# Scores of the first step's last pair of heads: sums over masked keys in place of gathered rows

## The chip, the core and the metric

The kernel runs on one core of a Trainium2 chip. The metric is the device time of one execution in microseconds (us).

The engines are PE (TensorE, matmuls), DVE (VectorE), ACT (ScalarE), POOL (GpSimd) and SP (SyncE, which here only issues DMA transfers). Each works through its own instructions in a fixed order, and waits where a result of another is missing.

## The reference

What is computed is a gated linear attention over 4 batches, 8 heads, 768 positions and 48 channels, followed by a layer of two matrix products:

```
f = 1 / (1 + exp(-f_logit))
for t in range(S):
    state = f[t][:, None] * state + outer(k[t], v[t])      # per batch and head, 48 x 48
    y[t] = q[t] @ state
x = y, all heads side by side                              # 3072 x 384
h = x @ w_in                                               # 384 -> 2048
g = where(h >= 1, h, where(h <= -1, 0, (h + 1) ** 2 / 4))
out = g @ w_out                                            # 2048 -> 384
```

The weights arrive as 64-bit floats, the rest as 32-bit.

## The kernel before, in words

**Steps and pairs.** The 768 positions are cut into 6 steps of C = 128 (`NI`). In each, the heads go by pairs (`NP` = 4): a pair has head 0 in partitions 0 to 47 and head 1 in 64 to 111. The first three pairs have one tile each, `kq[0]` to `kq[2]`, with keys in columns 0 to 511 and queries behind them. Partitions 48 to 63 and 112 to 127 of these tiles are free, and the fourth pair lies there, in thirds of 16 channels. `move` gathers those thirds by six DMA transfers into the tile `kq[3]`, half of them issued by SP and half by ACT.

**Gates.** `gate(m)` prepares one of three tiles per step (`NT` = 3): ACT takes the sigmoid; DVE runs a scan over the gates backwards (the tile `w`, line 471), takes its last column with a lower clamp of 1e-30 (`end`, line 474), its reciprocal (`rec`, 477), runs a scan forwards (478), and multiplies keys (480) and queries (482) by the two scans. The first tile of step 0 goes in two halves. POOL multiplies `end` by the first gate for a test of the range that the kernel makes (`least`, lines 494 and 496).

**Step 0.** It has no state yet, so its outputs are masked scores times values. `scores(n)` (594) makes, for pair n, the products of keys and queries of both heads in two PSUM banks, and two products on DVE with the mask (600) give `am`. `heads(t)` (821) and `thirds(t)` (832) multiply these by the values and gather x tile t in the bank `firsts[t]`: `heads` for the pairs' own heads, `thirds` for the pieces of the fourth pair. `rounded` (673 on ACT, 674 on DVE) writes each x as a sum of two reduced floats. `transpose_tensor` (654, with a copy to `kn` on ACT, 657) and `states` (762) prepare the state for step 1.

**Units.** The layer has 96 units, 16 (`NJ`) per step. `unit_1(k)` makes 128 rows of h for 512 columns by nine matmuls (236; for unit 0 line 863), ACT and DVE form g and split it (`act_1`, `act_2`, `act_3`, `ghi`, `glo`: 239, 242, 247, 250, 253), and `unit_2(k)` adds nine matmuls to the three output banks `po` (260), one unit behind.

**Weights.** `split_piece(k)` loads a piece of the weights into one of three buffers `raw`, and makes of it a high and a low part: ACT 364, DVE 366 (`bits`), ACT 369 (`w_hi`), DVE 370 (`w_lo`). A piece's load waits for line 366 of the piece three before. Units 0 to 3 have pieces of their own.

**What sets the order.** All this is written down as operations with costs and dependencies; `Plan.order` makes a list of it by a simulation with its cost table, and every engine, SP's DMA queue too, gets its instructions in that order. Where the plan leaves PE idle for more than 500 ns, `warm` (314) puts in matmuls of zeros, called fill here. Two tables, `TURNS` and `VISITS`, say beside which units the work of the later steps is put. The first step's work is put in by the lines 944 to 957 and 976 to 983.

## Time and profile before

| | |
|---|---|
| three runs | 484.01, 485.67 and 486.31 us; median 485.67 |
| the profiled execution | 484.96 us |
| its span, first to last instruction | 483.1 us |
| PE busy | 473.1 us (98%) |
| DVE busy | 372.5 us (77%) |
| ACT busy | 263.2 us (54%) |
| POOL busy | 22.1 us (5%) |
| HBM read | 44.63 MB |

All profile rows come from the profiled execution and are counted from the start of its span. Busy times of PE include fill. A timeline row that stands for several instructions gives their number behind the x; where they overlap, the time is that of all together. A matmul of 32-bit floats appears as two records. The middle column of a wait in brackets is the engine's idle time before the instruction, and what ended it.

### The profile page before, as it was taken

The page shows a single profiled execution, that of the slowest core. Times are in us where ns is not written, and L with a number is a line of the kernel's source. Part 1 is how long each engine was busy: PE and PEld are TensorE (multiplying, and loading weights), DVE is VectorE, ACT ScalarE, POOL GpSimd, SP SyncE. Part 2 cuts the span into 40 slices and gives each one's busy share as a digit, 9 for nine tenths or more (in the row PEclk, how much of TensorE's full clock was granted, in tenths as well). Part 3 has the DMA queues.
Part 4 walks back from the last instruction along what each step waited for, and adds up shares of the span by engine and source line. Part 5 has one row for each costly group of instructions (what it writes and reads, how often), then busy time and mean ns, then how long its engine had stood idle before and what let it go on. Part 6 is the DMA issues. An engine that isn't in the chain of part 4 may idle for free.

```text
span 483.1 us, 11267 instructions
## 1 busy us (share of the span) xinstructions
PE 473.1 (98%) x4664; PEld 385.1 (80%) x4664; DVE 372.5 (77%) x737; ACT 263.2 (54%) x483; POOL 22.1 (5%) x54
## 2 busy tenths in 40 slices
PE   8999999999999999999999999999999999999994
PEld 3678888889987887888887878888888888888883
DVE  7999878865899999999999589877667555655532
ACT  2489898754645455455555436464545444544451
POOL 3100001000100010110002000101000000000000
PEclk9999999999999999999999999999999999999998
DMA  8888644206502143013241413233410243422201
GB/s 305 262 305 294 229 136 144 73 3 231 156 2 89 68 117 96 31 36 121 88 127 39 152 45 122 67 109 79 152 45 3 88 114 96 156 86 86 85 0 71
DMA packets 21866, 54.48 MB, mean 113 GB/s; under 512 B 3472, under 2 KB 6672, under 8 KB 21808
## 3 DMA queue, kind: packets, MB, share of 16 engines
q1 hardware_dynamic: 20464, 51.53, 33.0%
q10 hardware_dynamic: 1344, 2.17, 1.9%
q8 instruction: 38, 0.62, 0.5%
q14 instruction: 20, 0.16, 0.1%
HBM read 44.63 MB, written 4.72 MB: 102 GB/s over the span
## 4 chain that ended last, share of the span: by engine, by line
PE 82%; DVE 7%; DMA 6%; ACT 2%; issue 1%; SPq 0%; DVEq 0%; ACTq 0%
PE po L260 38%; PE ph L236 36%; DMA raw<-in_w 5%; DVE kn L668 2%; PE pa L690 2%; PE pa L722 2%; PE ph L635 1%; DMA act<-in_f 1%; DVE act L247 1%; DVE w L471 1%; PE ph L783 1%; DVE glo L253 1%; PE pa L783 1%; ACT bits L364 1%; DVE f L478 1%
## 5 line engine op out<-in xcount | busy, mean ns | idle before, releaser
L236 PE MATMUL ph<-x,w_hi 128*128 128x512 f32 (+1 forms) x606 | 146.4, 377 | 0.0
L239 ACT ACTIVATE act<-ph,half 128x512 f32<-128x512 f32 x96 | 66.0, 687 | 115.8 <-PE ph L236 112.9
L236 PEld LDWEIGHTS ph<-x,w_hi 128*128 128x128 f32 x606 | 109.6, 188 | 21.1
L247 DVE SCALAR_TENSOR_TENSOR act<-ph,act 128x512 f32<-128x512 f32 x96 | 66.0, 687 | 59.9 <-ACT act L242 59.4
L250 ACT CAST ghi<-act 128x512 fp32r<-128x512 f32 x96 | 59.6, 621 | 66.2 <-DVE act L247 64.2
L260 PE MATMUL po<-ghi,w_hi 128*128 128x512 f32 (+1 forms) x306 | 87.0, 389 | 0.9 <-ACT ghi L250 0.8
L260 PE MATMUL po<-glo,w_hi 128*128 128x512 f32 (+1 forms) x306 | 83.5, 378 | 0.1
L260 PE MATMUL po<-ghi,w_lo 128*128 128x512 f32 (+1 forms) x306 | 83.4, 378 | 0.0
L236 PE MATMUL ph<-x,w_lo 128*128 128x512 f32 (+1 forms) x303 | 81.2, 376 | 0.0
L253 DVE TENSOR_TENSOR glo<-act,ghi 128x512 fp32r<-128x512 f32 x96 | 65.9, 686 | 16.0 <-ACT ghi L250 14.6
L668 DVE STREAM_TRANSPOSE kn<-kq 32x128 f32<-32x128 f32 x224 | 67.8, 303 | 3.5
L260 PEld LDWEIGHTS po<-glo,w_hi 128*128 128x128 f32 x306 | 55.3, 188 | 11.6 <-DVE glo L253 0.7
L260 PEld LDWEIGHTS po<-ghi,w_lo 128*128 128x128 f32 x306 | 55.4, 188 | 10.9
L236 PEld LDWEIGHTS ph<-x,w_lo 128*128 128x128 f32 x303 | 55.3, 188 | 10.4
L260 PEld LDWEIGHTS po<-ghi,w_hi 128*128 128x128 f32 x306 | 53.3, 188 | 12.4 <-ACT ghi L250 2.3
L242 ACT ACTIVATE act<-act 128x512 f32<-128x512 f32 x96 | 60.7, 632 | 3.0
L380 DVE TENSOR_REDUCE ok<-raw 128x1 f32<-128x512 f32 x48 | 31.3, 679 | 4.8 <-DMA raw<-in_w 4.8
L364 ACT ACTIVATE bits<-raw,top_of 128x512 uint32<-128x512 fp8e4 (+1 forms) x25 | 18.4, 742 | 9.7 <-DMA raw<-in_w 9.6
L471 DVE TENSOR_TENSOR_SCAN w<-f,ones 128x512 f32<-128x512 f32 (+1 forms) x21 | 21.3, 1016 | 2.4 <-ACT f L469 2.1
L478 DVE TENSOR_TENSOR_SCAN f<-f,rec 128x512 f32<-128x512 f32 (+1 forms) x21 | 21.3, 1020 | 0.5
L569 ACT ACTIVATE sd<-sd,kq 112x48 f32<-112x48 f32 x80 | 19.9, 327 | 0.0
L494 POOL TENSOR_TENSOR kq<-end,f0s 128x4 f32<-128x4 f32 (+1 forms) x21 | 4.9, 233 | 306.8 <-DVE end L474 227.4
(99 smaller groups left out, 377.7 us busy)
## 6 DMA issues: line engine op xcount, KB each, us to landing
raw<-in_w SPq DMA_DIRECT2D x24, 512.0 KB, 3.5
raw<-in_w SPq DMA_DIRECT2D x21, 511.6 KB, 4.4
kq<-in_kq SPq DMA_DIRECT2D x18, 512.0 KB, 4.9
out_y<-raw SPq DMA_DIRECT2D x18, 256.0 KB, 2.2
v<-in_v SPq DMA_DIRECT2D x10, 384.0 KB, 5.5
f<-in_f SPq DMA_DIRECT2D x13, 256.5 KB, 3.2
raw<-in_w SPq DMA_DIRECT2D x4, 382.9 KB, 5.4
kq<-kq SPq DMA_DIRECT2D x15, 64.2 KB, 3.0
```

The lines of the kernel that those rows point to most:

```text
L236: nc.tensor.matmul(ps[:, to], w_in(w_hi if high else w_lo, j, kt), xt[:, kt, t, c], start=(n == 0), stop=(n == 8))
L239: nc.scalar.activation(a, ps, AF.Relu, bias=half, scale=0.5)
L242: nc.scalar.activation(a, a, AF.Square)
L247: nc.vector.scalar_tensor_tensor(out=a, in0=ps, scalar=1.0, in1=a, op0=ALU.max, op1=ALU.min)
L250: nc.scalar.copy(hi, a)
L253: nc.vector.tensor_tensor(out=lo, in0=a, in1=hi.bitcast(F32), op=ALU.subtract)
L260: nc.tensor.matmul(po[e][:, c], w_out(part, j, e), g[:, of], start=(j == 0 and n == 0 and c.start == 0), stop=(j == NJ - 1 and n == 2))
L364: m = sca(COST["act"] * n // W, lambda: nc.scalar.activation(t, top, AF.Abs, bias=top_of, scale=2.0 ** 30), loaded, made[k - 4] if k >= 4 ...
L380: seen.append(vec("dve", lambda z=z, op=op: nc.vector.tensor_reduce(out=ok[:, 1 + NG + z + c:2 + NG + z + c], in_=words_of(raw[2])[1].bitc ...
L471: s1 = vec(1200 // count, lambda bwd=bwd, u0=u0, u1=u1: nc.vector.tensor_tensor_scan(out=wide(w[:, u0:u1]), data0=bwd, data1=wide(ones[:, ...
L478: s2 = vec(1200 // count, lambda fwd=fwd, b0=b0, b1=b1: nc.vector.tensor_tensor_scan(out=fwd, data0=fwd, data1=wide(rec[:, b0:b1]), initia ...
L668: nc.vector.transpose(kn[n % 2][u:u + 32, ::-1, r:r + 32], src[:, :, u:u + 32])
```

## The change

Four things change.

The last pair of step 0 gets its scores in another way. Its keys and queries are no longer gathered first. `scores_of_last(t)` lets ACT copy the keys of tile t with a scale that is 1 in the partitions of the last pair's thirds and 0 elsewhere (an extra column of `f0s`, which the host fills), and multiplies 32 rows of the copy, from partition 32 and from 96, with the queries of the same rows. The masked rows add nothing, and the sums over t = 0, 1, 2 gather in two banks. The copies lie in `kn`, which is free so early. The moves of step 0 take only the keys (512 columns, not 1028) and no longer wait for POOL.

Masks are an operation of their own (`masks`), and two tables, `START` and `AFTER`, set in which order the first step's operations are given to the plan. The transposes of pairs 0 and 1 come behind unit 0, those of pairs 2 and 3 behind unit 2's first layer. Banks and mask tiles are dealt out anew for this: pair 2 uses the second `ph` bank, in which fill was written, so no fill follows its scores until the units run.

The clamp becomes part of the first scan: where it multiplied and added a row of ones and zeros, it multiplies and takes the maximum with a row that holds 1 at a block's start and 1e-30 elsewhere. DVE's line 474 goes; the reciprocal reads `w` itself, and POOL copies the last column to `end`.

`TURNS` and `VISITS` are written out as tables; their numbers are the same.

```diff
+START = (("scores", 0), ("mask", 0), ("last", 0), ("scores", 1), ("mask", 1), ("last", 1), ("scores", 2), ("last", 2), ("mask", 2),
+         ("first", 0), ("first", 1), ("mask", 3), ("second", 3), ("second", 0), ("second", 1), ("second", 2))
+AFTER = {0: (("turn", 0), ("turn", 1)), 1: (("states", 0),), 2: (("turn", 2), ("turn", 3)), 3: (("states", 2),)}
...
-    def start_ones():
-        nc.vector.memset(ones, 0.0)
-        nc.vector.memset(ones[:, :, 0], 1.0)
+    def start_least():
+        nc.vector.memset(least_w, 1e-30)
+        nc.vector.memset(least_w[:, :, 0], 1.0)
...
             s1 = vec(1200 // count, lambda bwd=bwd, u0=u0, u1=u1: nc.vector.tensor_tensor_scan(
-                out=wide(w[:, u0:u1]), data0=bwd, data1=wide(ones[:, u0:u1]), initial=0.0,
-                op0=ALU.mult, op1=ALU.add), sg, None if split_up else c["sg"], set_ones, last)
-            en = vec("small", lambda b0=b0, b1=b1, u0=u0, u1=u1: nc.vector.tensor_scalar(
-                out=et[:, b0:b1], in0=w[:, u1 - 1:(u0 - 1 if u0 else None):-1, C - 1], scalar1=1e-30, scalar2=None, op0=ALU.max),
-                s1, of_half(m - 2, o, "pf"))
-            rc = vec("small", lambda b0=b0, b1=b1: nc.vector.reciprocal(out=rec[:, b0:b1, 0], in_=et[:, b0:b1]), en, last, set_rec)
+                out=wide(w[:, u0:u1]), data0=bwd, data1=wide(least_w[:, u0:u1]), initial=0.0,
+                op0=ALU.mult, op1=ALU.max), sg, None if split_up else c["sg"], set_least, last)
+            last_w = w[:, u1 - 1:(u0 - 1 if u0 else None):-1, C - 1]
+            en = add("POOL", "least", lambda b0=b0, b1=b1, last_w=last_w: nc.gpsimd.tensor_copy(
+                out=et[:, b0:b1], in_=last_w), s1, of_half(m - 2, o, "pf"))
+            rc = vec("small", lambda b0=b0, b1=b1, last_w=last_w: nc.vector.reciprocal(out=rec[:, b0:b1, 0], in_=last_w), s1, last, set_rec)
...
-            cols = slice(HW * h, HW * h + HW) if by_half else slice(0, 2 * N + B)
+            cols = slice(HW * h, HW * h + HW) if by_half else slice(0, 2 * N + B) if i else slice(0, N)
-                d = [o[a][h] for a in ("km", "qm", "pf")] if by_half else [o["km"], o["qm"], o["pf"][0]]
+                d = [o[a][h] for a in ("km", "qm", "pf")] if by_half else [o["km"], o["qm"], o["pf"][0]] if i else o["km"]
...
+    last_keys = [kn[0], kn[1], kn[0]]
+    am_of = [am[0:2], am[2:4], [act_f[0][:, 0:N].rearrange("r (b c) -> r b c", b=B), kn[1]], am[0:2]]
+    last_held = [bank(6), bank(4)]
+
+    def scores_of_last(t):
+        c = att[NP - 1]
+        c.setdefault("pt", [])
+        o = gates_of[t]
+        keys = sca("copy", lambda: nc.scalar.activation(wide(last_keys[t]), kq[t][:, 0:N], AF.Copy, scale=f0s[:, NI * NT * B:]), o["km"], ready["f0"], c["pt"][0] if t == 2 else [])
+        def emit():
+            for m in range(B):
+                for (_, ps, _), a in zip(last_held, (32, 96)):
+                    nc.tensor.matmul(ps[:, m], last_keys[t][a:a + 32, B - 1 - m], query(0, t, m)[a:a + 32], start=t == 0 and m == 0, stop=t == NT - 1 and m == B - 1)
+        c["sc"] = add("PE", "scores", emit, keys, o["qm"], [d for h in last_held for d in h[2]])
...
-    firsts = [bank(k) for k in (4, 5, 2)]
+    firsts = [bank(k) for k in (3, 2, 0)]
...
-        scores(n, ((0, 1), (2, 3), (0, 1), (3, 0))[n])
...
+    work = dict(mask=masks, scores=lambda n: scores(n, ((0, 1), (3, 2), (5, 7))[n]), last=scores_of_last, first=of_first, second=of_second,
+                turn=lambda n: transpose_tensor(n, {0: 1, 1: 5}.get(n)), states=lambda n: states(n))
+    for kind, n in START:
+        work[kind](n)
...
-        if u == 0:
-            states(0)
-        elif u == 1:
-            for n in (2, 3):
-                transpose_tensor(n)
-        elif u == 2:
-            states(2)
+        for kind, n in AFTER.get(u, ()):
+            work[kind](n)
...
+    last = (np.arange(128) % 64 >= 48).astype(np.float32)
+    f0 = np.concatenate([f0, last[:, None]], 1)
```

Three places show how the instructions stand. The first is DVE in the gates of the second and third tile. `w` is the backward scan, `f_1` and `act_1` the gates, `kq_0` and `kq_1` the tiles of keys and queries. Before:

```order
L471 SCALAR_TENSOR_TENSOR w_73<-f_1_67,ones_64 128x512
L474 TENSOR_SCALAR end_1_75<-w_73 128x4
L477 RECIPROCAL rec_65<-end_1_75 128x4
L478 SCALAR_TENSOR_TENSOR f_1_67<-f_1_67,rec_65 128x512
L480 TENSOR_TENSOR kq_1_69<-kq_1_69,w_73 128x512
L482 TENSOR_TENSOR kq_0_68<-kq_0_68,f_0_66 128x256 x2
L471 SCALAR_TENSOR_TENSOR w_73<-act_1_84,ones_64 128x512
```

And in the changed kernel:

```order
L480 SCALAR_TENSOR_TENSOR w_73<-f_1_67,least_w_64 128x512
L491 TENSOR_TENSOR kq_0_68<-kq_0_68,f_0_66 128x256 x2
L486 RECIPROCAL rec_65<-w_73 128x4
L487 SCALAR_TENSOR_TENSOR f_1_67<-f_1_67,rec_65 128x512
L489 TENSOR_TENSOR kq_1_69<-kq_1_69,w_73 128x512
L480 SCALAR_TENSOR_TENSOR w_73<-act_1_84,least_w_64 128x512
```

The clamp is gone from the row, and the queries of the first tile come ahead of the reciprocal.

The second place is DVE behind the gates. `am` are masked scores, `bits` and `w_lo` the splits of weights; three masks stand ahead of it in both. Before:

```order
L600 TENSOR_TENSOR am_3_79<-po0_115,mask_101 128x512
L366 SCALAR_TENSOR_TENSOR bits_0_95<-raw_0_92,bits_0_95 128x384
L366 SCALAR_TENSOR_TENSOR bits_1_96<-raw_1_93,bits_1_96 128x384
L370 TENSOR_TENSOR w_lo_100<-bits_0_95,w_hi_99 128x3x128
L370 TENSOR_TENSOR w_lo_100<-bits_1_96,w_hi_99 128x3x128
L600 TENSOR_TENSOR am_0_76<-pa0_110,mask_101 128x512
L600 TENSOR_TENSOR am_1_77<-pa1_111,mask_101 128x512
L366 SCALAR_TENSOR_TENSOR bits_2_97<-raw_2_94,bits_2_97 128x512
L600 TENSOR_TENSOR am_2_78<-po0_115,mask_101 128x512
L600 TENSOR_TENSOR am_3_79<-pa0_110,mask_101 128x512
```

And in the changed kernel:

```order
L635 TENSOR_TENSOR am_3_79<-pa2_112,mask_101 128x512
L635 TENSOR_TENSOR act_0_83<-po2_117,mask_101 128x512
L635 TENSOR_TENSOR kn_1_81<-ph1_114,mask_101 128x512
L375 SCALAR_TENSOR_TENSOR bits_0_95<-raw_0_92,bits_0_95 128x384
L635 TENSOR_TENSOR am_0_76<-ph0_113,mask_101 128x512
L375 SCALAR_TENSOR_TENSOR bits_1_96<-raw_1_93,bits_1_96 128x384
L635 TENSOR_TENSOR am_1_77<-po1_116,mask_101 128x512
```

The masks of pair 2 (into `act_0` and `kn_1`) follow at once, and two splits, not five, stand ahead of the last mask.

The third place is PE from the end of unit 0 to the second layer of unit 0. `ph` are the banks of h, `pa` those of attention, `sd` the values. Before:

```order
L863 MATMUL ph0_113<-x_0_85,w_hi_99 128x512 x2
L762 MATMUL pa0_110<-sd_82,kn_0_80 48x48 x8
L762 MATMUL pa0_110<-sd_82,kn_1_81 48x48 x8
L236 MATMUL ph1_114<-x_0_85,w_hi_99 128x512 x6
L236 MATMUL ph1_114<-x_0_85,w_lo_100 128x512 x3
L654 MATMUL pa1_111<-ident_103,kq_2_70 128x112 x4
L654 MATMUL pa2_112<-ident_103,kq_3_71 128x112 x4
L260 MATMUL po0_115<-ghi_0_88,w_hi_99 128x512
```

And in the changed kernel:

```order
L898 MATMUL ph0_113<-x_0_85,w_hi_99 128x512 x2
L689 MATMUL pa1_111<-ident_103,kq_0_68 128x112 x4
L689 MATMUL po2_117<-ident_103,kq_1_69 128x112 x4
L245 MATMUL ph1_114<-x_0_85,w_hi_99 128x512 x6
L245 MATMUL ph1_114<-x_0_85,w_lo_100 128x512 x3
L797 MATMUL pa0_110<-sd_82,kn_0_80 48x48 x8
L797 MATMUL pa0_110<-sd_82,kn_1_81 48x48 x8
L269 MATMUL po0_115<-ghi_0_88,w_hi_99 128x512
```

The transposes of pairs 0 and 1 have come in behind unit 0; those of pairs 2 and 3 now stand behind unit 2's first layer.

## Rows read from the trace of the kernel before

**Rows 1.** The page: busy time, share of the span and instructions of each engine.

```profile
PE 473.1 (98%) x4664; PEld 385.1 (80%) x4664; DVE 372.5 (77%) x737; ACT 263.2 (54%) x483; POOL 22.1 (5%) x54
```

**Rows 2.** PE's timeline: start, us, instruction and number, idle before.

```profile
12.27 1.16 PE L594 MATMUL pa<-kq 48*128 48x128 f32 x16
...
17.25 1.97 PE L821 MATMUL po<-am,sd 128*64 128x128 f32 x32
...
24.50 1.07 PE L832 MATMUL po<-am,v 128*32 128x128 f32 x16
...
27.75 0.48 PE L863 MATMUL ph<-x,w_lo 128*128 128x512 f32 x1
...
29.98 0.93 PE L762 MATMUL pa<-sd,kn 128*48 128x48 f32 x32
30.84 1.66 PE L236 MATMUL ph<-x,w_hi 128*128 128x512 f32 x6
...
33.02 0.93 PE L654 MATMUL pa<-ident,kq 112*128 112x112 f32 x8
34.58 0.96 PE L260 MATMUL po<-ghi,w_hi 128*128 128x512 f32 x3 [0.64 <-ACT ghi L250]
...
46.00 1.52 PE L236 MATMUL ph<-x,w_hi 128*128 128x512 f32 x6
```

**Rows 3.** Fill behind unit 0: one row of PE's timeline, and the group.

```profile
144.27 1.25 PE L314 MATMUL po<-zeros 128*128 128x512 bf16 x5
...
L314 PE MATMUL po<-zeros 128*128 128x512 bf16 x15 | 3.9, 382 | 0.0
```

**Rows 4.** DVE's timeline, 7 to 24 us.

```profile
7.07 1.23 DVE L471 TENSOR_TENSOR_SCAN w<-f,ones 128x512 f32<-128x512 f32 x1
8.33 0.17 DVE L474 TENSOR_SCALAR end<-w 128x4 f32<-128x4 f32 x1
8.54 0.18 DVE L477 RECIPROCAL rec<-end 128x4 f32<-128x4 f32 x1
...
11.15 1.22 DVE L471 TENSOR_TENSOR_SCAN w<-act,ones 128x512 f32<-128x512 f32 x1
...
12.87 0.16 DVE L474 TENSOR_SCALAR end<-w 128x4 f32<-128x4 f32 x1
13.06 0.18 DVE L477 RECIPROCAL rec<-end 128x4 f32<-128x4 f32 x1
13.28 1.23 DVE L478 TENSOR_TENSOR_SCAN act<-act,rec 128x512 f32<-128x512 f32 x1
...
15.60 1.88 DVE L600 TENSOR_TENSOR am<-pa,mask 128x512 f32<-128x512 f32 x3
...
17.99 1.02 DVE L366 SCALAR_TENSOR_TENSOR bits<-raw,bits 128x384 uint32<-128x384 uint32 x2
...
22.80 0.68 DVE L600 TENSOR_TENSOR am<-pa,mask 128x512 f32<-128x512 f32 x1
```

**Rows 5.** ACT's timeline: a sigmoid, a piece of weights, a cast.

```profile
6.37 0.63 ACT L469 ACTIVATE f<-f 128x513 f32<-128x513 f32 x1 [2.51 <-DMA f<-in_f]
...
32.01 0.76 ACT L364 ACTIVATE bits<-raw,top_of 128x512 uint32<-128x512 fp8e4 x1 [0.57 <-DMA raw<-in_w]
...
41.80 0.62 ACT L369 CAST w_hi<-bits 128x512 fp32r<-128x512 f32 x1
```

**Rows 6.** POOL's timeline, 11 to 15 us.

```profile
11.01 0.26 POOL L496 COPY f0s<-kq 128x4 f32<-128x4 f32 x1
...
13.37 1.11 POOL L496 COPY f0s<-kq 128x4 f32<-128x4 f32 x1
```

**Rows 7.** Stretches: length; busy us (instructions) of each engine; PE's granted clock; DMA share, GB/s.

```profile
0.00:5.00 5.00, 3.33 (x8) 1.19 (x9) 2.21 (x9) 2.12 (x3) 1.84 (x12) 1.00 0.59 179
5.00:10.00 5.00, 5.00 (x23) 2.19 (x22) 4.79 (x11) 1.41 (x3) 0.75 (x1) 1.00 1.03 394
...
45.00:50.00 5.00, 5.00 (x24) 4.14 (x23) 4.97 (x10) 4.97 (x9) 0.71 (x2) 1.00 0.79 253
```

More of the change, by code (lines that the diff above doesn't have):

```diff
@@ L154, in gla_moe @@
     zeros = const.tile([128, 128], BF16, name="zeros")
-    ones = const.tile([128, B, C], F32, name="ones")
+    least_w = const.tile([128, B, C], F32, name="least_w")
     rec = const.tile([128, B, C], F32, name="rec")
@@ L399, in split_again @@
         nc.vector.tensor_tensor(out=w_lo[:, c], in0=val, in1=w_hi[:, c].bitcast(F32), op=ALU.subtract)
-    banks = {k: [] for k in range(6)}
+    banks = {k: [] for k in range(8)}
     turn = {"n": 0}
@@ L409, in bank @@
             turn["n"] += 1
-        return k, (pa[k] if k < 3 else po[k - 3].rearrange("p (b c) -> p b c", b=B)), banks[k]
+        return k, (pa[k] if k < 3 else (po + ph)[k - 3].rearrange("p (b c) -> p b c", b=B)), banks[k]
     pairs = [(i, p) for i in range(NI) for p in range(NP)]
@@ L584, in scores @@
     def scores(n, at):
-        i, p = pairs[n]
         c = att[n]
@@ L590, in emit @@
         def emit():
+            if 7 in at:
+                opened["bank"] = None
             for m, (q, b) in enumerate(blocks(n)):
@@ L596, in scores, with masks @@
         c["sc"] = add("PE", "scores", emit, c["kq"], [d for h in held for d in h[2]])
+        c["held"] = held
+    last_keys = [kn[0], kn[1], kn[0]]
[11 more added lines that the diff above has]
+        c["sc"] = add("PE", "scores", emit, keys, o["qm"], [d for h in last_held for d in h[2]])
+        c["pt"].append(c["sc"])
+        c["held"] = last_held
+    def masks(n):
+        c = att[n]
         c["am"] = []
-        for h, (b, ps, _) in enumerate(held):
-            t = am[n % 2 * 2 + h]
+        for h, (b, ps, _) in enumerate(c["held"]):
+            t = am_of[n][h]
             o = vec("dve", lambda t=t, ps=ps: nc.vector.tensor_tensor(
                 out=t, in0=ps, in1=mask.rearrange("u (o t) -> u o t", o=1).broadcast_to([C, B, C]), op=ALU.mult),
-                c["sc"], ready["mask"], old(n - 2, "y"))
-            banks[b] = [o]
+                c["sc"], ready["mask"], att[0]["ys"][h] if n == 3 else att[3]["pt"][1] if n == 2 else [])
+            banks[b][:] = [o]
             c["am"].append(o)
@@ L927, in compare @@
         def compare():
-            nc.vector.tensor_scalar(out=ok[:, 1:1 + NG], in0=f0s, scalar1=LEAST, scalar2=None, op0=ALU.is_ge)
+            nc.vector.tensor_scalar(out=ok[:, 1:1 + NG], in0=f0s[:, 0:NG], scalar1=LEAST, scalar2=None, op0=ALU.is_ge)
             most = ok[:, 1 + NG + 2 * NW:]
@@ L946, in gla_moe, with of_first, of_second @@
         prepare(n)
-        scores(n, ((0, 1), (2, 3), (0, 1), (3, 0))[n])
-        if n == 1:
-            for t in range(2):
-                att[0]["y"] = att[1]["y"] = heads(t, lambda m, e, t=t: va[:, m, 2 * e + t], am[t::2], [att[e]["am"][t] for e in range(2)], att[0]["lv"])
-    for n in (0, 1):
-        transpose_tensor(n, (1, 3)[n])
-    two = [att[n]["am"] for n in (2, 3)]
-    heads(2, lambda m, e: vb[:, m, 64 * e:64 * e + 64], am[0::2], [a[0] for a in two], [att[2]["lv"], att[1]["am"]])
-    for t in range(NT):
-        y = att[2]["y"] = att[3]["y"] = thirds(t, am[1::2], [a[1] for a in two])
+    def of_first(t):
+        att[0].setdefault("ys", []).append(heads(t, lambda m, e: va[:, m, 2 * e + t], [am_of[e][t] for e in range(2)], [att[e]["am"][t] for e in range(2)], [att[0]["lv"], banks[firsts[t][0]]]))
+        att[0]["y"] = att[1]["y"] = att[0]["ys"][-1]
+    def of_second(t):
+        two = [att[n]["am"] for n in (2, 3)]
+        if t == NT:
+            heads(2, lambda m, e: vb[:, m, 64 * e:64 * e + 64], [am_of[n][0] for n in (2, 3)], [a[0] for a in two], [att[2]["lv"], att[1]["am"], att[0]["am"]])
+            return
+        y = att[2]["y"] = att[3]["y"] = thirds(t, [am_of[n][1] for n in (2, 3)], [a[1] for a in two])
         x_of[0, t] = rounded(firsts[t][0], wide(firsts[t][1]), x[0][:, t, 0], x[0][:, t, 1], y, None)
+    work = dict(mask=masks, scores=lambda n: scores(n, ((0, 1), (3, 2), (5, 7))[n]), last=scores_of_last, first=of_first, second=of_second,
+                turn=lambda n: transpose_tensor(n, {0: 1, 1: 5}.get(n)), states=lambda n: states(n))
+    for kind, n in START:
+        work[kind](n)
     for k in range(len(order)):
@@ L962, in gla_moe @@
     groups = {}
-    TURNS = {4: 7, 5: 8, 6: 14, 7: 14}
-    VISITS = {4: (8, 9, 10), 6: (14, 15, 16)}
-    for i, (first, second) in enumerate((((5, 8, 9), (9, 12, 13)), ((0, 4, 6), (6, 10, 12)), ((-4, 4, 6), (6, 10, 12)), ((-4, 4, 6), (6, 10, 12))), 2):
-        for n, at in ((NP * i, first), (NP * i + 2, second)):
-            VISITS[n] = [NJ * (i - 1) + u for u in at]
-            TURNS[n] = TURNS[n + 1] = VISITS[n][0]
     for n, u in TURNS.items():
```

10 lines of the change are left out of this document (6 added, 4 removed).

## The prediction, made before the result was known

> **What bounds the kernel now.** I read the page first: TensorE (PE) is busy 473.1 us of the 483.1 us span [rows 1]. A count that includes filler says little about where time can be won, so I went to PE's timeline. It has two parts. Up to 24.50 us PE runs scores, heads and fill; from then on it runs thirds, units and attention nearly without a gap, to the end. The last visible wait of the head is the one of 0.64 us at 34.58, for ACT's ghi of unit 0 [rows 2]. Behind it, fill is nearly the only thing on PE that is not work: 15 matmuls, 3.9 us [rows 3]. So time is won by bringing forward the moment at which thirds and units can start, or by taking work off PE behind it; nothing else moves the end.
>
> What sets that moment is DVE's timeline [rows 4]: it works through the three gates from 7.07 to 15.60 without a gap, then takes eight mask products between the first four splits of weights. The last pair of masks comes late (22.80), because its scores wait for rows that are gathered by DMA behind the gates.
>
> **The change part by part.** The sum is made against the profiled execution: 483.1 us span, 484.96 us in all. That execution lies 0.71 us under the median of the three runs, 485.67 us; I add the 0.71 at the end.
>
> *The clamp.* Two clamps of a whole gate leave DVE's row: 8.54 - 8.33 = 0.21 and 13.06 - 12.87 = 0.19 [rows 4]. The clamps of the first half-gates save nothing: the scan at 7.07 has its input only when ACT's sigmoid ends at 6.37 + 0.63 = 7.00 [rows 5]. So the masks can start at 15.60 - 0.40 = 15.20. The scan itself now takes a maximum where it added. No row shows that. The nearest below is an ordinary pass over 512 columns, 0.68 us; above, a scan and such a pass, 1.91 us. I take the scan's own 1.23 [rows 4], which it is nearest to, since only one of the two operations of the same instruction changes; the ends stay in the range, at two scans (7.07 and 11.15) times -0.55 and +0.68, so -1.1 to +1.4 us.
>
> *The copies on POOL.* The clamped value that the test reads becomes a POOL copy, 22 in all. The next gate's scan waits for it. In the head that scan (11.15, 0.2 sooner now) comes 2.6 us after the copy can start (8.30), and the longest such copy takes 1.11 us [rows 6]: hidden [rows 4]. If that cover failed, each gate would be late by at most 1.1 us. The row also shows who pays when both engines read: the POOL copy of 4 columns took 1.11 us at 13.37 instead of 0.26, while the DVE scan of 13.28 took the usual 1.23 [rows 4, 6]. [...]
>
> *The masked keys.* ACT gets three copies of 128x512, 0.63 us each [rows 5], at about 9, 11 and 15 us, where it mostly waits for weights: hidden. PE gets three groups of eight matmuls in place of one. A group takes 1.16 us [rows 2]; the new ones multiply over 32 rows instead of 48, but over as many columns, so I take the same 1.16. The first two groups run while DVE is in the gates. The third follows the scores of pair 2: from 15.3 two groups of 1.1 end at 17.5, two heads of 0.95 (1.97 for both) at 19.4 [rows 2]. The moves of the gathered rows stay on SP and ACT, now for transposes alone and with half the bytes; they wait for the keys only, so SP's queue and the weight load behind them are released a little sooner.
>
> *DVE's masks.* Six masks at (17.99 - 15.60) / 4 = 0.60 us, from 15.20 to 18.79; a split of 0.51 (1.02 for two), the last pair's first mask, a split, its second mask: this one ends at 21.0 [rows 4]. On PE the third head waits for the first of those masks (20.0) and takes 0.95: also 21.0. So thirds start at 21.1 instead of 24.50, **3.4 us sooner**. Splits of the third and fourth weight piece come 1 us later than before; at the units they are wanted after 30 us, so this costs nothing unless the second rival holds.
>
> *Units.* Thirds take 27.75 - 24.50 = 3.25, unit 0 29.98 - 27.75 = 2.23, the eight transposes of pairs 0 and 1, now behind it, 34.58 - 33.02 - 0.64 = 0.92 (price of the other eight), unit 1 33.02 - 30.84 = 2.18, the states between them 0.86 [rows 2]. 21.1 + 9.4 = 30.5 for the second layer of unit 0, against 34.58. Its ghi must be there: unit 0 ends at 26.6; 0.69 + 0.63 on ACT, 0.69 on DVE, 0.61 on ACT with some 0.3 of hops make 29.5, and two copies and a cast that stand between hardly more than 29.9. Before, that cast stood behind two weight pieces that ACT waited for (32.01, [rows 5]); now only one late piece is ahead of act_1. So 4.1 us are won there. But the transposes of pairs 2 and 3, which lay ahead of 34.58 before, come next on PE: 0.92 back. **Gain up to here 3.1 us.**
>
> *Fill.* The order shows 51 fill matmuls instead of 71: 29 instead of 56 ahead of unit 0, where PE waits anyway, but 22 instead of 15 behind. Seven at 0.26 us (3.9 us for 15 [rows 3]) are 1.8 us if PE would have worked, nothing if it would have waited there. I take **1.3 us back**, nearer to the full price, because PE is almost never idle in the rows before. Behind 35 us the tables of turns and visits hold the same numbers as before.
>
> **Sum:** 3.1 - 1.3 = 1.8 us. 484.96 - 1.8 = 483.2 in a run like the profiled one, and with 0.71 the median is **483.9 us**.
>
> **Rivals.**
> 1. *The extra fill lies in waits.* The order puts fill where PE was expected to be idle, and the row of five at 144.27 lay in front of attention that needed DVE. Against it: only 15 were needed before, at the same places. Then the gain is the full 3.1 us: 482.6.
> 2. *The weights become the bound.* Between 45 and 50 us ACT is busy 4.97 of 5 us and DVE 4.97 [rows 7]. Unit 4 starts at 46.00 [rows 2], and the last piece that it multiplies by first is cast at 41.80 + 0.62 = 42.42 [rows 5]: 3.6 us of slack. A start 3.1 us sooner uses almost all of it, and the splits start later than before. If ACT and DVE, which have no room, can't bring them forward, PE waits there, and the gain shrinks to some 0.3: 485.4.
> 3. *The clock falls*, and the kernel is slower. Fill ahead of unit 0 goes from 56 to 29, with none after the scores of pair 2, so PE has pauses between 8 and 15 us that were filled before. At the start, eight matmuls took 3.33 us where later 23 took 5.00: 0.42 against 0.22 each, though the row gives the clock as 1.00 [rows 7]. [...] It decides with the first group of scores behind a pause, if that takes twice 1.16. [...] By the rows it is not likely: the pauses come to under 1 us each (fill to about 8.2, scores at 9.1; keys' sums and fill to 12.3, scores at 12.8).
> 4. *DVE waits for POOL's copies:* four in the head at 0.26 us [rows 6], 1.0 us on DVE's path: 484.9.
> 5. *The last pair was not late for its rows:* if heads or casts and not masks set the thirds, nothing is won and the transposes cost: 485.7.
>
> **How the numbers follow.** My forecast 0.46, the rivals in their order 0.24, 0.15, 0.06, 0.05 and 0.04. The range takes in the first rival with part of the scan's lower end, and the second and fourth: 481.8 to 486.1; the clock is left out. A measurement can tell about 0.5%, 2.4 us, from no change. Under 483.2 lie most of the first rival and a third of my own case: 0.36. Over 488.1 lie the clock and a corner of the second: 0.08. The rest, 0.56, is within.
>
> **What would show it.** Right: in the changed profile the masks start near 15.2, the last mask ends near 21, thirds near 21.1, unit 0 at 24.4, its second layer near 30.5; no PE wait between 36 and 90 us beyond a few tenths; the scan keeps 1.23. Wrong: a PE wait for ACT or DVE at unit 4 (rival 2), fill rows with a wait still behind them (rival 1), matmuls of 0.42 us before unit 0 (rival 3), DVE rows that stretch beside a POOL copy (rival 4).

## The result, and the profile after

The changed kernel takes **486.85 us** (median of 22 runs, 484.42 to 492.26), the kernel before 484.49 us (22 runs, 483.58 to 486.31). The ratio is 1.0043, its 95% interval 1.0028 to 1.0058: slower by some 2 us, where 1.8 us less were forecast. The median lies 0.75 us above the upper end of the forecast's range.

The profiled execution of the change took 485.0 us with a span of 483.2, as long as the one of before [rows 1]. But the two spans are made up differently: the last matmul of the second layer starts 1.25 us later than in before (476.84 against 475.59), and what follows it, copies and output transfers, was 1.1 us shorter in this execution; over all profiles of this document that tail lies between 5.9 and 7.2 us. The page's row of busy times:

```profile
PE 472.3 (98%) x4676; PEld 385.7 (80%) x4676; DVE 369.4 (76%) x715; ACT 264.4 (55%) x486; POOL 30.3 (6%) x76
```

The head went as forecast. DVE's timeline (start, duration, instruction), then PE's: first third, first matmul of unit 0, its second layer.

```profile
7.05 1.22 DVE L480 TENSOR_TENSOR_SCAN w<-f,least_w 128x512 f32<-128x512 f32 x1 [0.37 <-ACT f L478]
...
15.24 0.69 DVE L635 TENSOR_TENSOR am<-pa,mask 128x512 f32<-128x512 f32 x1
...
20.37 0.68 DVE L635 TENSOR_TENSOR am<-po,mask 128x512 f32<-128x512 f32 x1
```

```profile
21.05 0.30 PE L867 MATMUL po<-kn,v 128*32 128x128 f32 x1
...
24.35 0.48 PE L898 MATMUL ph<-x,w_lo 128*128 128x512 f32 x1
...
30.29 0.96 PE L269 MATMUL po<-ghi,w_hi 128*128 128x512 f32 x3
```

Masks start at 15.24 (forecast 15.2), thirds at 21.05 (21.1), unit 0 at 24.35 (24.4), its second layer at 30.29 (30.5). Against 34.58 of before [rows 2] that is a lead of 4.29 us. Following the lead over all 918 matmuls of the second layer: it is 2.75 where before is at 52 us (1.5 gone, the transposes behind the first units among them), 3.57 at 137, 2.19 at 189, 1.49 at 264. Then it falls in two steps, by 1.3 us to 0.17 near 292 and by 1.35 to -1.23 near 366, and stays there. PE's waits between 280 and 370 us (total, times, longest) and its timeline around the first step:

```profile
PE pa L670 <- issue: 1.0, 1, 1.0
PE ph L670 <- issue: 1.0, 1, 1.0
```

```profile
290.65 0.22 PE L670 MATMUL pa<-kq 48*64 48x64 f32 x1
291.86 0.27 PE L670 MATMUL ph<-kq 48*64 48x64 f32 x1 [0.99 <-issue]
```

PE stops in the middle of a group of scores for which everything is there: no semaphore holds it ("issue"). Before has no such row. Second, the other runs differ from the profiled one. The eleven with a mean granted clock of 0.995 or more took 484.42 to 486.89 us (median 485.79); the nine at 0.984 to 0.994 took 486.81 to 490.0; the two at 0.981 and 0.982 took 492.26 and 492.04 and count as slow, so the ratio leaves them out. The runs of before that stood beside the experiments had 0.995 or more.

So three things had to be explained: the stalls, the clock, and the lead lost between 140 and 265 us.

### The profile page after: what moved, and what is told of

The parts are those of the page before. It is cut to its first block, busy times and chain, and to the rows that moved or that the text cites. A ratio compares the mean times of both kernels' runs of the same rounds, so it can differ in the third digit from the quotient of the medians.

```text
span 483.2 us, 11296 instructions
## 1 busy us (share of the span) xinstructions
PE 472.3 (98%) x4676; PEld 385.7 (80%) x4676; DVE 369.4 (76%) x715; ACT 264.4 (55%) x486; POOL 30.3 (6%) x76
## 4 chain that ended last, share of the span: by engine, by line
PE 77%; DVE 13%; ACT 3%; DMA 3%; issue 2%; SPq 1%; DVEq 0%
PE po L269 36%; PE ph L245 33%; DVE kn L703 4%; PE pa L725 2%; PE pa L757 2%; DVE w L480 1%; DVE glo L262 1%; DMA f<-in_f 1%; PE ph L670 1%; DMA raw<-in_w 1%; DVE f L487 1%; DVE act L256 1%; DVE kq L491 1%; PE pa L818 1%; ACT bits L373 1%
## 5 line engine op out<-in xcount | busy, mean ns | idle before, releaser
L245 PEld LDWEIGHTS ph<-x,w_hi 128*128 128x128 f32 x606 | 109.6, 188 | 21.1
L484 POOL COPY end<-w 128x4 f32<-128x4 f32 (+1 forms) x22 | 6.8, 310 | 271.0 <-DVE w L480 270.9
L480 DVE TENSOR_TENSOR_SCAN w<-f,least_w 128x512 f32<-128x512 f32 (+1 forms) x21 | 21.2, 1015 | 2.8 <-ACT f L478 2.5
```

What stands on the lines that cost most here:

```text
L245: nc.tensor.matmul(ps[:, to], w_in(w_hi if high else w_lo, j, kt), xt[:, kt, t, c], start=(n == 0), stop=(n == 8))
L480: s1 = vec(1200 // count, lambda bwd=bwd, u0=u0, u1=u1: nc.vector.tensor_tensor_scan(out=wide(w[:, u0:u1]), data0=bwd, data1=wide(least_w[ ...
```

## The experiments

Medians of 4 to 22 runs in us; before's own runs stood beside each, and the ratios are to those. "Late fills" are the fills behind the units (22 in the change, 15 in before), "pages moved" means that the number of PE's instructions is changed without other work, "the clamp's order" is explained with e14.

| run | what it is | us | ratio to before, 95% |
|---|---|---|---|
| the change | | 486.85 | 1.0043 (1.0028 to 1.0058) |
| e1 | no fill behind the units | 483.27 | 0.9973 (0.9949 to 0.9996) |
| e2 | head's pauses filled | 485.49 | 1.0012 (0.9998 to 1.0027) |
| e3 | pages moved | 483.35 | 0.9970 (0.9952 to 0.9988) |
| e4 | before, pages moved the other way | 488.93 | 1.0077 (1.0055 to 1.0099) |
| e5 | e2 and e3 together | 483.50 | 0.9968 (0.9951 to 0.9985) |
| e6 | e2, no late fill | 482.48 | 0.9940 (0.9917 to 0.9963) |
| e7 | 8 instructions fewer | 485.29 | 1.0010 (0.9990 to 1.0031) |
| e8 | before with the third part alone | 486.48 | 1.0036 (1.0021 to 1.0050) |
| e9 | e5 with the clamp back | 482.14 | 0.9945 (0.9928 to 0.9963) |
| e10 | e6 with the clamp back | 481.46 | 0.9935 (0.9914 to 0.9955) |
| e11 | e3, less fill in the head | 488.01 | 1.0066 (1.0043 to 1.0088) |
| e12 | e8, reciprocal behind the copy | 486.16 | 1.0028 (1.0015 to 1.0040) |
| e13 | before, copies alone | 485.03 | 0.9989 (0.9975 to 1.0002) |
| e14 | before, third part in before's order | 484.63 | 0.9983 (0.9966 to 1.0000) |
| e15 | e6 in the clamp's order | **479.99** | 0.9896 (0.9867 to 0.9924) |
| e16 | e5 in the clamp's order | 481.11 | 0.9915 (0.9885 to 0.9945) |

### The stalls: pages of 256 instructions

The page's row for queue 8 of the changed kernel (packets, MB, share), and the same row for 289.4 to 289.6 us, 1.2 us ahead of the first stall:

```profile
q8 instruction: 38, 0.62, 0.5%
```

```profile
q8 instruction: 1, 0.02, 29.1%
```

Queue 8 brings instructions in packets of 0.62 MB / 38 = 16 KB while the kernel runs. From the packet ahead of the first stall to the one ahead of the second (289.50 and 364.49 us) there are six, and PE executes 1536 records from stall to stall: 256 for each packet. I call 256 such records an instruction page, or a page for short in what follows on stalls; PE's 9411 make 37. Where three kinds of attention work meet (lines L757, L725, L670 of the changed kernel) PE executes 320 weight loads and matmuls in 2.3 us: a page lasts under 2 us. My theory was that PE runs dry if a whole page lies inside such a group, which the number of instructions ahead of it decides, whatever they do.

*e3* leaves the work as it is and changes that number by 230, which is 26 fewer modulo 256 (before has 27 fewer than the change):

```diff
-            if opened["bank"] is not None:
+            if opened["start"] and parted[0] < 23:
+                parted[0] += 1
+                for z in range(6):
+                    c = slice(85 * z, 85 * z + 85)
+                    nc.tensor.matmul(opened["bank"][:, c], zeros, zeros[:, 0:85], start=True, stop=True)
+            elif opened["bank"] is not None:
```

> The changed kernel with the same fill of the head in more pieces (23 fills of 512 columns become 138 of 85), that is 230 instructions more ahead of everything, which is 26 fewer if instruction pages of 256 decide. Theory A (pages): no stall released by 'issue' in the dense groups, the profiled execution 2.4 us shorter, 482.4 to 483.2 at a clock of 0.997; everything up to 290 us unchanged within 0.3. Rival F (the stalls come from the work itself: a semaphore, the banks, the order): both stalls stay and the time is 484.5 to 485.5 at that clock. If the lower clock of half of the runs comes from the stalls, it is gone too; if from the head, it stays.

*e4* does the same to before, 13 fills as two of 256 columns each, 26 instructions more:

> The kernel before with 13 of the head's fills each as two of 256 columns: 26 TensorE instructions more and no other work, so that its dense groups stand against the instruction pages about as those of the change do. Theory A (pages): two stalls of 1.2 us released by 'issue' appear near 291 and 365, the time is 486.5 to 487.5 against 484.5. Rival F (the stalls come from the changed work): no stall, 484 to 485. If the stalls are also what lowers the clock in other runs, a part of the runs has a clock under 0.993 and lies at 488 or more; if not, all runs stay within 1.5 us of each other.

e3 has no stall left and took 483.35 us. e4 got both. Its waits (total, times, longest):

```profile
PE pa L642 <- issue: 1.3, 1, 1.3
PE ph L642 <- issue: 0.9, 1, 0.9
```

Its price was larger than forecast, 3.7 us: 2.9 us of lead go at the two places. Its profiled run loses more elsewhere: the second layer of unit 0 comes 1.2 us later than in before (ACT waited 2.44 us for a piece of weights at 24.34; in e13, which has before's instructions on PE, it comes 1.05 us later too), and 1.7 us go between 136 and 184 us, which I have not taken apart. But a kernel that works without a stall got both by 26 fill instructions. More telling than the times is where PE stops. The stretch view counts what had started when PE stood still: first field the stretch, then its length, then busy time and instructions of PE and of its weight loads. The change, then e4:

```profile
0.00:291.50 291.50, 288.00 (x3275) 234.03 (x3275) 254.56 (x514) 174.17 (x330) 27.28 (x70) 1.00 0.42 134
0.00:366.50 366.50, 362.04 (x4040) 295.18 (x4040) 310.46 (x619) 211.86 (x401) 30.30 (x76) 1.00 0.40 125
```

```profile
0.00:296.00 296.00, 291.84 (x3275) 236.03 (x3276) 256.08 (x530) 172.44 (x326) 19.32 (x50) 1.00 0.41 129
0.00:371.00 371.00, 365.81 (x4041) 297.17 (x4042) 311.15 (x636) 210.23 (x398) 21.84 (x54) 1.00 0.39 121
```

Two kernels with other work ahead stop at the same instruction: 3275 matmuls and 3275 or 3276 loads, then 4040 or 4041. With the semaphore records, PE had started 6593 and 8129 records in both, 6 x 256 apart. The times in the trace fit a page that is too short. In the change PE starts the first record of the page that ends at the stall at 288.78 us; the packet begins 0.72 us later (289.50), and PE goes on at 291.86, 3.1 us after the page's start. In before the two pages that begin at the same records as those of the change last 4.0 us (from 290.48) and 3.6 us (from 364.10), and PE doesn't stop. This gave a sharp forecast: *e7* takes 8 instructions away (2 fills in place of 6 before 262 us), which is more than the 6 that the first group had left at its stall and less than the 12 of the second.

```diff
-                    warm(int((o.start - idle) * 0.9 / (330 if o.start < 10000 else 230)))
+                    count = int((o.start - idle) * 0.9 / (330 if o.start < 10000 else 230))
+                    warm(count if count != 6 else 2)
```

> The changed kernel with 2 fills in place of 6 before the unit at 262 us: 8 TensorE instructions fewer ahead of both dense groups. In three profiles with stalls TensorE stopped at the same instruction, the 6593rd and the 8129th record, 1536 = 6 x 256 apart; the group at 290 us of the change ends 6 records after the first, the group at 365 us 12 records after the second. Theory A says therefore: exactly one stall, none at 290, one of 1.2 us at 365 with 4 records of the group left; 1.2 us less than the change at the same clock, 483.6 to 484.6 in the runs at 0.997. Rival: both stalls stay or both go.

```profile
PE pa L670 <- issue: 1.3, 1, 1.3
...
PE po L269 <- issue: 0.5, 1, 0.5
```

One stall in a group, the second one, with exactly 4 records of the group left. What I had not expected is the second row: at the first place PE still lost 0.5 us, now at the matmuls right behind the group. The time: 485.29 us over ten runs; the six at a clock of 0.995 or more took 484.18 to 485.39 (median 484.85), a little over the 483.6 to 484.6 forecast.

### The clock: pauses in the head

*e2* adds five fills:

```diff
         def emit():
+            warm((0, 1, 2)[n])
             if 7 in at:
...
         def emit():
+            warm(2 if t == 0 else 0)
             for m in range(B):
```

> The changed kernel with 5 more fills in the head's pauses of TensorE (before the first masked scores 2, before the scores of pair 1 one, of pair 2 two). Theory D (the runs of the change at 487 to 490 us have a lower mean granted clock, 0.984 to 0.991, because TensorE pauses in the head, which before has not): with the pauses filled all runs have a clock of 0.996 or more and lie at 484.5 to 486, so the median is 1.5 us lower than the change's 486.85. Rival E (the clock falls for another reason, such as the stalls at 290 and 365 or the few fills after the head): half of the runs stay at a clock under 0.993, median 486 to 488. The two stalls stay in either case (10 instructions more).

All 12 runs had a clock of 0.995 to 0.999, none above 486.88 us (three lie above the 486 forecast); median 485.49, with both stalls. Theory D held. What happens without the fills, e3's profile shows, which fell on a run with a clock of 0.989 (486.0 us). PE's timeline, then stretches of PE alone (busy, instructions, granted clock, DMA share, GB/s):

```profile
13.69 0.37 PE L611 MATMUL po<-kq 48*128 48x128 f32 x1 [0.99 <-DVE kq L498]
...
16.22 0.58 PE L611 MATMUL po<-kq 48*128 48x128 f32 x1 [0.28 <-DVE kq L498]
```

```profile
12.00:14.00 2.00, 1.01 (x8) 1.00 1.03 365
14.00:16.00 2.00, 1.94 (x32) 1.00 0.77 227
16.00:18.00 2.00, 1.78 (x16) 0.51 0.32 59
18.00:20.00 2.00, 2.00 (x20) 0.50 0.68 247
...
22.00:24.00 2.00, 2.00 (x32) 0.78 0.84 263
```

PE waited 0.99 us for DVE at 13.69, and at 16 us the granted clock fell to 0.50 and stayed there until 22 to 23 us; the matmuls from 16.22 on take 0.42 in place of 0.27. Here the second layer of unit 0 came 3.2 us later than in the profiled run of the change, and nothing made up for it. e2 in the same stretch never left 1.00. *e11* turns the dose the other way: e3 without the four fills between the masked scores and the scores of pair 1 (`and not 10000 < o.start < 16000` behind the fill's condition).

> The changed kernel with the pages moved (as in the run in more pieces), and without the 4 fills that stand between the masked scores and the scores of pair 1: TensorE's pause there grows by 0.9 us. Theory D (pauses in the head lower the clock): most of the runs have a clock of 0.992 or less and lie at 485 to 487; with the fills 3 of 12 did, and with 5 more none. Rival E (the clock falls by chance or elsewhere): the share of such runs stays at 1 in 4 and the median at 483 to 483.8.

All five runs had 0.982 to 0.986 and took 486.31 to 489.01 us: more than I expected. Its longest wait and its stretches:

```profile
PE po L611 <- DVE kq L498: 1.9, 1, 1.9
```

```profile
12.00:14.00 2.00, 0.81 (x7) 0.64 1.06 376
14.00:16.00 2.00, 2.00 (x18) 0.50 0.56 167
...
22.00:24.00 2.00, 2.00 (x22) 0.50 0.85 267
```

Runs at 0.992 or less: none of 52 with five fills more (e2, e5, e6, e9, e10, e15, e16), 19 of 56 with the head of the change (10 of 22, and 2, 3 and 4 in e1, e3 and e7), 5 of 5 with four fewer. The fill in the head's pauses decides it. How long a single pause must be is not shown. The profiled run of e7 (0.992) has the head of the change and fell as e3's did:

```profile
14.00:16.00 2.00, 1.72 (x28) 1.00 0.94 308
16.00:18.00 2.00, 2.00 (x20) 0.57 0.20 44
18.00:20.00 2.00, 2.00 (x22) 0.50 0.69 254
```

Its pauses ahead of that were 0.49, 0.43 and 0.28 us; those of the change's profiled run, which kept 1.00, were 0.31, 0.28 and 0.28.

### The lead lost between 140 and 265 us

My first suspect was the 22 fills behind the units, which stand in the changed kernel's groups (number, total us, mean ns of one) with GpSimd's copies:

```profile
L484 POOL COPY end<-w 128x4 f32<-128x4 f32 (+1 forms) x22 | 6.8, 310 | 271.0 <-DVE w L480 270.9
...
L323 PE MATMUL po<-zeros 128*128 128x512 bf16 x22 | 5.8, 382 | 0.0
```

*e1* leaves them out (`and opened["start"]` in the fill's condition):

> The changed kernel without the 22 fills behind the units (the fills of the head stay). In the profiled execution of the change the lead over before, 4.3 us at 30.3, had shrunk to about 2.2 at 183 and to 1.5 at 262 where groups of fills stand, and two stalls of TensorE of 1.2 us each (290.65 and 365.70, released by 'issue') took the rest. Theory A (fills cost close to their full time, stalls come from where instruction pages begin, which 44 instructions fewer move): the fills' 22 x 0.23 = 5.0 us go down by what lay in waits, a gain of 2 to 4 us, the stalls at 290 and 365 are gone (2.4 us more), 479 to 482 us at a granted clock of 0.997. Theory B (the fills only lie in waits): no gain from them, 482.5 to 485. Theory C (the fills hold the clock): the granted clock falls under 0.99 and the time is 486 or more. If the two stalls stay at their places in the dense groups, the theory of the instruction pages is in doubt.

483.27 us without a stall, as e3 with all 22 fills (483.35); e1 had one run at a clock of 0.981 and three at 0.992 or 0.993. Against Theory A, 5 us of fill were worth next to nothing, and in its profile PE waits for DVE where they had stood:

```profile
141.49 0.67 PE L725 MATMUL pa<-am,v 64*48 64x64 f32 x32 [0.72 <-DVE am L676]
...
143.21 0.25 PE L818 MATMUL ph<-v,kn 64*48 64x48 f32 x2 [0.98 <-DVE act L256]
...
146.34 0.96 PE L269 MATMUL po<-glo,w_hi 128*128 128x512 f32 x3 [0.62 <-DVE glo L262]
```

With the head filled, e6 against e5 (below), leaving them out was worth 1.0 us. So the fills mark the lost time and make at most a part of it. They also do something that I overlooked: in e6's profiled run (0.993), which has none, the granted clock fell to 0.50 at 143.3 us, behind two such waits (0.73 and 0.98 us), and was back at 146.7. What makes the lost time? *e8* puts the third part alone into before:

```diff
-                op0=ALU.mult, op1=ALU.add), sg, None if split_up else c["sg"], set_ones, last)
-            en = vec("small", ... nc.vector.tensor_scalar(out=et[:, b0:b1], ..., scalar1=1e-30, scalar2=None, op0=ALU.max), ...)
-            rc = vec("small", ... nc.vector.reciprocal(out=rec[:, b0:b1, 0], in_=et[:, b0:b1]), en, last, set_rec)
+                op0=ALU.mult, op1=ALU.max), sg, None if split_up else c["sg"], set_ones, last)
+            en = add("POOL", "least", ... nc.gpsimd.tensor_copy(out=et[:, b0:b1], in_=last_w), ...)
+            rc = vec("small", ... nc.vector.reciprocal(out=rec[:, b0:b1, 0], in_=last_w), s1, last, set_rec)
```

> The kernel before with the third part of the change alone: the scan's max with 1e-30 in place of the clamp, the copy on GpSimd, and nothing else; the program itself then has 22 fills behind the units in place of 15, as the change has. 24 of the head's fills stand in 6 pieces so that the pages lie as in before (254 instructions more). Theory H (the waits between 140 and 262 us that take 2 us of the lead come from this part, since GpSimd's copy comes later than VectorE's clamp did or the order of VectorE's work is another): 486 to 487, 1.3 to 2 us over before, the loss at 147 to 189 and at 263 us. Rival (the part is free, the loss comes from the moved scores or the earlier units): 484.3 to 485.2.

486.48 us: the part that I had booked as a gain of 0.4 us in the head makes before 1.7 us slower, with the change's 22 late fills. In its profile the lead over before falls by 0.7 us near 147, by 1.1 between 183 and 199, by 0.6 at 263 and by 0.5 between 300 and 310. The second layer of unit 0 starts 0.9 us late there too, but so it does in e13 with before's order (1.05). The change without it, *e9*, with the diff of e8 turned round in e5's kernel:

> The kernel of the run with both remedies (head's pauses filled, pages moved), with the clamp on VectorE back in place of the scan's max: the first two parts of the change without the third. Fills behind the units are 15 again, as in before. Theory H (the third part costs 1.3 to 2 us in any kernel of this kind): 481.4 to 482.4, 1.3 to 2 us under the 483.5 with it, 2.4 to 3.4 under before, and the lead over before at 310 us is 3.3 or more in place of 1.8. Rival (the price of the third part belongs to before's head): 483 to 484.

482.14 us, 1.4 less than e5 (0.0023 in ratios, 1.1 us; the intervals overlap); its lead at 310 us was 2.72 (expected 3.3) against e5's 1.69. So the price belongs to the third part; its cause could be POOL's copies or the order. *e12* lets the reciprocal wait for the copy (`s1, en, last, set_rec`):

> The kernel before with the third part of the change, but the reciprocal waits for GpSimd's copy as it waited for the clamp in before. Work is the same as in the run with the third part alone (486.48); only VectorE's order differs: a unit's product with its activation comes between the scan and the reciprocal again, as in before, not after the reciprocal and the second scan. Theory I (the third part costs because the reciprocal and the second scan follow the first scan at once and a unit's product, for which TensorE waits, comes 1.4 us later): 484.3 to 485.2, no difference from before. [...]

486.16 us: Theory I's number (484.3 to 485.2) was missed, and Rival J's, 486 to 487 because GpSimd's copies themselves cost, was hit. The profile shows a long wait on ACT's queue: the issues of three moves, waiting themselves, stand ahead of a unit's activation. They stand there in before too, where they take 2.37 us.

```profile
176.67 5.35 ACTq L278 DMA_DIRECT2D x<-y  x3
...
182.06 0.69 ACT L239 ACTIVATE act<-ph,half 128x512 f32<-128x512 f32 x1 [5.57 <-DMA v<-in_v]
...
185.40 1.37 PE L260 MATMUL po<-ghi,w_hi 128*128 128x512 f32 x3 [2.61 <-ACT ghi L250]
```

Right behind it the granted clock was 0.50, from 185.7 to 189.1 us. But the profiled run was the slowest of the twelve (488.38 us); whether the others had this wait isn't shown. e12 changed the planner's order once more and settled nothing. Two kernels that keep before's order did: *e13* keeps the clamp, into a tile that nobody reads, and adds the max and the copies (22 by the page, 21 in the texts below); *e14* also drops the clamp, but the planner still sees a step of its cost:

```diff
+            gap = vec("small", lambda: None, s1, of_half(m - 2, o, "pf"))
...
-            rc = vec(..., s1, last, set_rec)
+            rc = vec(..., s1, gap, last, set_rec)
```

> The kernel before with the scan's max and GpSimd's 21 copies, and with the clamp kept on VectorE into a spare tile, on which the reciprocal still waits (it reads the scan's result). Every engine but GpSimd then has before's instructions in before's order, and the pages lie as in before. Rival J (the third part costs through GpSimd's copies): 486 to 487. Theory I (it costs through the order that the planner makes without the clamp): 484.3 to 485.3, no difference from before.

> The kernel before with the third part whole (no clamp, 21 copies on GpSimd), but the planner still sees a step of the clamp's cost between scan and reciprocal that emits nothing, so that every engine keeps before's order and the 15 fills. Theory I: 484.0 to 485.2, nothing lost, and of the 21 x 0.16 = 3.4 us of clamps on VectorE at most a few tenths gained, since TensorE waits for VectorE in few places. Rival J: 486 to 487, as in the run with the third part alone (486.48).

485.03 and 484.63 against 485.29: the copies cost nothing that can be measured, nor does the max; the order does. The same place in DVE's timeline of before, of e8, then of e14:

```profile
259.61 1.22 DVE L471 TENSOR_TENSOR_SCAN w<-f,ones 128x512 f32<-128x512 f32 x1
260.74 0.67 DVE L247 SCALAR_TENSOR_TENSOR act<-ph,act 128x512 f32<-128x512 f32 x1
261.32 0.16 DVE L474 TENSOR_SCALAR end<-w 128x4 f32<-128x4 f32 x1
261.52 0.18 DVE L477 RECIPROCAL rec<-end 128x4 f32<-128x4 f32 x1
```

```profile
260.97 1.22 DVE L478 TENSOR_TENSOR_SCAN w<-f,ones 128x512 f32<-128x512 f32 x1
262.22 0.18 DVE L484 RECIPROCAL rec<-w 128x4 f32<-128x4 f32 x1
262.44 1.22 DVE L485 TENSOR_TENSOR_SCAN f<-f,rec 128x512 f32<-128x512 f32 x1
263.58 0.67 DVE L247 SCALAR_TENSOR_TENSOR act<-ph,act 128x512 f32<-128x512 f32 x1
```

```profile
258.23 1.22 DVE L471 TENSOR_TENSOR_SCAN w<-f,ones 128x512 f32<-128x512 f32 x1
259.39 0.69 DVE L247 SCALAR_TENSOR_TENSOR act<-ph,act 128x512 f32<-128x512 f32 x1
260.00 0.17 DVE L478 RECIPROCAL rec<-w 128x4 f32<-128x4 f32 x1
260.20 1.23 DVE L479 TENSOR_TENSOR_SCAN f<-f,rec 128x512 f32<-128x512 f32 x1
```

In e14 the unit's product comes 1.16 us after the scan's start, between scan and reciprocal, as it does in before (1.13). In e8 it comes 2.61 us after it, behind the second scan. PE waits for what is made from this product. At the same place, without late fills in either, e6 and then e15, which has e14's empty step:

```profile
262.31 0.50 PE L269 MATMUL po<-glo,w_hi 128*128 128x512 f32 x1 [0.40 <-DVE glo L262]
```

```profile
260.48 0.39 PE L269 MATMUL po<-glo,w_hi 128*128 128x512 f32 x1
```

The planner takes, among the steps that are ready when an engine comes free, the one that is due first. In its list of e8 the product is ready at this place only after the first scan's end, so the reciprocal and the second scan are taken, though the product is due earlier; with the clamp's step it is ready in time.

### All together

*e5* has e2's fills and 22 fills in six pieces each; *e6* and *e10* have e2's fills and none behind the units, e10 with the clamp back; *e16* and *e15* are e5 and e6 with e14's empty step.

> The changed kernel with both remedies: 5 more fills in the head's pauses, and 22 of the head's fills in 6 pieces each, which brings the count of TensorE instructions ahead of the dense groups to 230 more (no page of 256 begins and ends in a group). Theory: the forecast of the change was right but for two terms, the stalls by instruction pages (2.4 us) and the clock that falls where TensorE pauses in the head. Then all runs have a clock of 0.995 or more, no run is above 485, and the median is 482.6 to 483.4, 1.6 to 2.4 us under before. Rival: the head's gain is taken by other waits as soon as the stalls are gone: 484 to 485, no difference from before.

> The changed kernel with 5 more fills in the head's pauses and without the 22 fills behind the units (34 instructions fewer, so no stall by pages). Theory G (the late fills lie in waits for VectorE, 0.3 us of them at most costs anything; the lead of the change is lost between 140 and 262 us to those waits): 481.8 to 483, at most 1 us under the kernel with both remedies, and waits of 0.5 to 1 us for VectorE stand where the fills were. Rival (a fill costs its 0.23 us): 3 to 5 us under it, 478 to 480. Rival C (the late fills hold the clock): runs with a clock under 0.993 remain, at 484 to 488.

> The changed kernel with the clamp back, the head's pauses filled and no fill behind the units (3 instructions fewer than before's alignment, so no stall by pages). With the max the late fills cost 1.0 us (483.5 against 482.5 without them); with the clamp there are 15 in place of 22, so they can cost 0.5 to 0.8: 480.6 to 481.8, the fastest of all. Rival C (the late fills hold the clock): runs under 0.993 appear, 483 or more.

> The changed kernel with the head's pauses filled, the pages moved, the 15 late fills and the empty step: it differs from the run with both remedies (483.5) by the planner's order alone. Theory I: 481.4 to 482.5, as with the clamp back (482.14). Rival J: 483 to 484.

> The changed kernel with the head's pauses filled, no fill behind the units, and the empty step between scan and reciprocal: all three parts of the change, in the order that the clamp gave. Theory I: as the run with the clamp back and no late fill (481.46) or up to 0.7 less, 480.6 to 481.8. Rival J: as the run with the max and no late fill, 482.5 or more.

e5 came out at 483.50, 0.1 over its forecast, with every clock at 0.996 or more, one run at 485.15; e6 at 482.48, e10 at 481.46, e16 at 481.11. **e15, 479.99 us, beats both kernels**: 1.0% under before. e16 and e15 lie under their forecasts, by 0.3 and 0.6 us. The late fills cost 1.1 us (e16 against e15, four and six runs, intervals overlapping), and without them no run of e6, e10 or e15 has a mean clock under 0.993.

In ratios to before, each a kernel against the next: the three parts in a good order, with pages and pauses mended, -0.0085 (e16), some 4.1 us won; the order without the clamp +0.0053 (e16 to e5), 2.6 us; the pages +0.0044 (e5 to e2), 2.1 us; the pauses +0.0031 (e2 to the change), 1.5 us. With the intervals of the table these sizes are rough; but the pages (e4, e7), the pauses (e11) and the order (e8 against e14) each stand on a second set of runs too. The order isn't the seven more late fills in disguise: e6 and e15 have none, and differ by 0.0044, 2.1 us (the intervals just overlap). With the order kept, taking the clamp off VectorE seems to win something (0.0030 from e9 to e16, 0.0039 from e10 to e15, 0.0017 in e14), but the intervals overlap.

## Why the prediction was wrong

- **The units' start** was right: 3.4 us sooner was forecast for unit 0, 27.75 - 24.35 = 3.4 came; for the second layer 4.1 and 4.29. e15 kept 3.74 us of that to its last matmul (4.21 at first), e16 3.49 (3.52).
- **The clamp** was the step that failed first. "Two clamps of a whole gate leave DVE's row" counts the work that goes, 0.4 us in the head, and takes the places of all other steps as given; "Behind 35 us the tables of turns and visits hold the same numbers as before" put the order of DVE behind the head at nothing. The order without the clamp cost 2.6 us (e16 to e5; e8 cost before 1.7). The scan's max was right: 1.22 us.
- **Fill:** "Seven at 0.26 us", taken as 1.3 us back, took a sign of the loss for its cause. The seven more came from the third part alone (e8 has 22 as well), and behind them stood the late products. The listing of the order, which I used to count the fills, would also have shown where VectorE's product had gone; I read TensorE's rows and not VectorE's.
- **A missing term:** the number of PE's instructions. Nothing in the forecast asked what 27 more of them do; they cost 2.1 us (e5 to e2). The profile of before couldn't show it: its second dense group ended 15 records short of the instruction at which the others stopped.
- **Rival 3, the clock,** was the right mechanism with a chance of 0.06, and rejected for "under 1 us each". Pauses of 0.99 us (e3) and of 0.49 us and less (e7) were followed by the fall. It struck half of the change's runs, nine of them at 1 to 4 us and two at 6, and only six of these eleven lie over 488.1 us, where I had looked for it: it did not hold through the whole head, in e3 only from 16 to between 22 and 23 us. It cost the median 1.5 us (e2 to the change).
- **Rival 1** (fill lies in waits) is nearer the truth than my own price: all 22 cost 1.0 us (e5, e6) of their 5.8. **Rival 2** didn't come: PE waited 0.19 us for ACT at 44.95, no more. **Rival 4** is refuted by e13: its 22 copies on GpSimd cost nothing that could be measured (ratio 0.9989, 0.9975 to 1.0002). **Rival 5** fell with the head; its 485.7 left out the 1.3 us of fill.
- **The base:** 0.71 us were added for a median of three runs, 485.67. Over 22 runs before has 484.49, so the same sum from there would have been 482.7, and the miss is larger than it looks.

## What to carry to other kernels

When an order is computed from costs and readiness, taking out a short instruction is a change of order first; compare the order of every engine that others wait for, and if the old one was better keep the step as an empty place. Where small matmuls run in hundreds, look for "issue" in TensorE's waits and for the instruction fetches, and move the count by a few dozen before you believe a difference of half a per cent. A kernel whose runs scatter needs the clock of each run, not only that of the profiled one.

## What the runs showed that I had not expected

- PE stopped 1.2 to 1.5 us when a dense group held a page of 256 instructions, at the same instruction in four kernels; 26 instructions without work made before 3.7 us slower (2.9 of it at the two places in its profile).
- PE's granted clock fell to 0.50 behind a pause of 0.99 us (e3) or three of 0.28 to 0.49 us (e7) among small matmuls of 32 and 48 rows, in which PE reads as busy 1.94 of 2 us (e3); with five fills in the pauses no mean clock of 52 runs was under 0.993. It also fell in mid-kernel, behind waits of 0.73 and 0.98 us where fill had been left out (e6).
- A move's issue that waits on ACT's queue held a unit's activation behind it for 5.57 us, in the slowest of e12's runs.
